# Low parts of weights and activations from Pool to VectorE, and range checks from layer 1 to layer 2

## The chip, the cores and the metric

One core of one Trainium2 chip runs the whole program; the other cores of the chip run nothing of it. The metric is the device time of one execution in microseconds, and a kernel's time is the median of its runs. TensorE (PE in the profile), VectorE (DVE), ScalarE (ACT), GpSimd (POOL, called Pool here) and SyncE (SP, which issues the DMAs) each work through a queue of their own in order and wait for one another by semaphores. TensorE's granted clock is printed as a share of full speed: 1.00 is 2.4 GHz, 0.50 is 1.2 GHz.

## The reference

A recurrence over 768 tokens (4 batches, 8 heads of 48 columns) gives the input of two layers of 384 to 2048 to 384 columns each, one with an ELU, one with a sigmoid gate. All of it in float32:

```python
for t in range(S):                                    # attention
    cur = np.einsum('bhd,bhe->bhde', u[None] * kt, vt)
    y[:, :, t] = np.einsum('bhd,bhde->bhe', rt, state + cur)
    state = wt[:, :, :, None] * state + np.einsum('bhd,bhe->bhde', kt, vt)
x = y.transpose(0, 2, 1, 3).reshape(3072, 384)
h = x @ w_in;  x = np.where(h > 0, h, np.exp(np.minimum(h, 0)) - 1) @ w_out     # layer 1
h = x @ w2_in; x = (h * (1 / (1 + np.exp(-1.702 * h)))) @ w2_out                # layer 2
```

The weights arrive as float64, in pairs of 32-bit words.

## The kernel before

**Layers.** The 3072 tokens go in 6 tiles of 512. A layer's 2048 inner columns are 16 blocks of 128 (index f). `layers` runs 192 steps j: first 6 tiles of 16 steps for layer 1 (j from 0 to 95), then the same for layer 2 (96 to 191). Step j issues on TensorE the 9 products of h for block f of its tile (L145) and among them the output products of the block two steps back (9 of layer 1, L176; 12 of layer 2, L185). Each float32 value is used as a high part (rounded by a ScalarE cast) and a low part (the value less its high part): three products stand for one. `split_g` makes the two parts of a step's activation g: the cast is L168, the subtraction L169. h has two PSUM banks, and e, g and hl two buffers each.

**Weights.** One block's weights (in and out, 128x768 pairs of words) are loaded (`load_w`), turned into float32 by bit operations on VectorE (`bits_w`: L100 or L104 and L106, then L110 twice) and split by `parts_w`: cast on ScalarE (L134), subtraction on Pool (L135). Layer 1's 16 blocks are made in the first tile, two steps ahead of their use; two of them before the first step, beside the attention's first chunks (`lead`). Layer 2's take their places and are made from step `turn` = 82 on, at 8/3 VectorE operations a step.

**Range checks.** Layer 1's weights are made as if all were in float32's range. That is checked later: half blocks are loaded again (`see`, L115 to L117) and looked at by one ScalarE square and three VectorE passes (`check`, L124 to L128), one half a step, in steps 5 to 15 of layer 1's later tiles. Layer 2's weights are checked as they are made: a ScalarE square with an accumulator (L87), a compare (L104) and a masked shift (L106). The decays are checked by `flags`, two ScalarE passes a chunk with accumulators (L262, L263), while the chunk's decays lie in memory. All leave their results in the columns of two small tiles, which `verdict` sums up once in layer 2; a second path for any inputs (`any_decay`) would run after it and does not with these inputs.

**Attention.** 24 chunks of 128 tokens, four stages each, one stage a step beside layer 1; four chunks and a stage come before the first step. Pool makes keys, queries and bonus products (L270, L278, L330, L331, L343) and a key's low part (L306); VectorE the scans (L242, L249), masks and state.

**The order** is written out by hand (a manual schedule): what a step's code issues in this order goes into each engine's queue in this order.

```python
        issue(mm, among, late)                       # TensorE: the step's products
        if j >= 1:
            making = j <= NF or j >= turn and state["parts"] < len(order)
            hls[j - 1] = moe.split_g(gs.pop(j - 1), TILE, nc.gpsimd if making else nc.vector)
```

Then come the step's share of the weights, `soon` (attention), `act` (the activation of h), `after` (attention, or the verdict), `parts_w` in the first tile, `see` and `check`, and at a tile's second step the copies of the finished tile out of PSUM (L514 in layer 1; in layer 2 L523, two on VectorE and two on ScalarE, each followed by its DMA). Layer 2's next input is loaded at f = 3 to 5 and split at f = 4 to 6.

Of the kernel before, what the change touches and what calls it, by code (L numbers as in the profile page):

```python
# [12 lines left out]
F32 = mybir.dt.float32  # L13
# [38 lines left out]
class Moe:  # L52
    """Two products with an activation between them, tokens along the free dimension."""
# [11 lines left out]
    # float64 weights, as pairs of words, to the high and the low part of a float32.  # L65
    #
    # A float64's high word holds sign, 11 bits of exponent and 20 of mantissa. In the range of
    # normal float32 numbers its exponent's bits 9 to 7 are all the opposite of bit 10, so taking
    # them out and moving the rest leaves the float32. As float32 patterns the high words are in
    # order of size: one comparison of squares finds those below the range, of which no bits are  # L70
    # moved; numbers above it are clamped, or counted for the caller.

    def later(self, layer):
        return self.large is not None and layer == 1

    def sq_w(self, layer, f):
        nc = self.nc
        if self.later(layer):
            return
        hf = self.raw[layer, f][:, 1].bitcast(F32)  # L80
        t = self.t[layer, f] = self.p["tmp"].tile([P, 2 * DM], F32, tag="tmp", name="wt")
        if self.large is None:
            nc.vector.tensor_scalar(out=hf, in0=hf, scalar1=-HIGH_MAX, scalar2=HIGH_MAX, op0=ALU.max, op1=ALU.min)
            nc.scalar.activation(t, hf, AF.Square)
        else:
            i = 2 * NF + f
            nc.scalar.activation(t, hf, AF.Square, accum_out=self.large[:, i:i + 1])  # L87
# [3 lines left out]
    def bits_w(self, layer, f):  # L91
# [3 lines left out]
        if self.later(layer):  # L95
            t = self.t[layer, f] = self.p["tmp"].tile([P, 2 * DM], F32, tag="tmp", name="wt")
        t = self.t[layer, f]
        ti = t.bitcast(I32)
        if self.later(layer):
# [12 lines left out]
    # The first layer's weights are made in a hurry, as if all were in the range or zeros. That is  # L112
    # looked after later, half a block at a time.

    def see(self, src, k):  # L115
        raw = self.t["seen", k] = self.p["tmp"].tile([P, 2 * DM], I32, tag="tmp", name="seen")
        self.nc.sync.dma_start(raw, src[k // 2][:, k % 2 * 2 * DM:(k % 2 + 1) * 2 * DM])  # L117
# [12 lines left out]
    def parts_w(self, layer, f):  # L130
# [4 lines left out]
        nc.gpsimd.tensor_tensor(out=w[:, 1, :], in0=t, in1=w[:, 0, :].bitcast(F32), op=ALU.subtract)  # L135

    def h(self, layer, f, x, n):
        """PSUM [f rows, tokens] of x @ w_in, and the products that fill it."""
# [11 lines left out]
    def act(self, layer, h, n):  # L150
# [3 lines left out]
        if layer == 1:  # L154
            # exp(min(h, 0)) - 1 = -relu(1 - exp(h)); elu = max of it and h
# [9 lines left out]
    def split_g(self, g, n, engine):  # L165
# [3 lines left out]
        engine.tensor_tensor(out=hl[:, 1, :n], in0=g[:, :n], in1=hl[:, 0, :n].bitcast(F32), op=ALU.subtract)  # L169
# [25 lines left out]
class Attention:  # L195
    """A chunk of tokens at a time, all heads. With E the decays' product before a token and I
    with its own, token t takes r_t E_t . (k_s / I_s) of v_s from the tokens s of its chunk, and
    r_t E_t of the state before the chunk; the state after it is I of the last token times what
    (k / I)^T v adds up to. The flags tell where the decays leave the bounds in which no product
    of a chunk can leave the range of float32."""  # L200
# [14 lines left out]
    def room(self, c, what, rows, cols):  # L215
        """For what is loaded; before the layers, in the places of the last of their weights."""
# [9 lines left out]
    def psum(self, what):  # L226
        """A bank; the second layer's tags are free as long as there is only attention."""
# [7 lines left out]
    def decay(self, c):  # L235
        """Products of the decays, in both directions."""
# [15 lines left out]

    def flags(self, c):
        if c >= NCH or "flags" in self.t[c]:
            return
        nc = self.nc
        self.t[c]["flags"] = True
        w = self.t[c]["w"][:, :NP * SEG].rearrange("p (s t) -> p s t", t=SEG)[:, :, 1:]
# [22 lines left out]
    def block(self, c, copy=None):  # L281
        """The queries of each head apart from those of the other one of its pair, in their parts once
        the weights are made."""
# [185 lines left out]
def layers(nc, moe, w1, w2, x2d, out, x_of, beside, lead):  # L469
# [67 lines left out]
    for j in range(STEPS):  # L537
# [27 lines left out]
        if moe.large is not None and NF < j < turn and f >= CALM and seen <= 2 * NF:  # L565
            # in the middle of a tile
            if seen < 2 * NF:
                moe.see(w1, seen)
# [317 lines left out]
```

## Time and profile before

Three runs took 1038.16, 1040.42 and 1041.01 us, median 1040.42. One execution was profiled; its instructions span 1036.9 us (its time outside the span is not recorded, the runs' times hold it).

| | |
|---|---|
| time, median of 3 | 1040.42 us |
| span of the profiled execution | 1036.9 us |
| TensorE busy | 978.0 us, 94% |
| its weight loads | 831.6 us, 80% |
| VectorE | 700.7 us, 68% |
| ScalarE | 457.3 us, 44% |
| Pool | 313.0 us, 30% |
| subtractions for weights' low parts, Pool, L135 | 32 of 2120 ns |
| for activations' low parts, L169 | 44 on Pool of 1670 ns, 148 on VectorE of 742 ns |
| checks of weights, `seen` loads | 32 of 384 KB, 3.4 us to landing |

A share of the whole span says little here, since the program runs through stretches with different limits: the table of stretches in the rows below gives each engine's busy time in microseconds, and how near that is to the length of the stretch. The list of groups gives for each line and shape a count, the busy time and the mean duration; where that mean is well above the shortest of the same shape, something held the instruction.

### The profile page before, as it was taken

To read this page: it belongs to the slowest core of one execution; us is meant where nothing else is said; L and a number is where in the kernel's file an instruction comes from. 1 tells how busy PE (TensorE), PEld (TensorE's weight loads), DVE (VectorE), ACT (ScalarE), POOL (GpSimd) and SP (SyncE) were. 2 spreads that over 40 slices of the span, in tenths; PEclk is the share of its full clock that TensorE was granted. 3 is DMA by queue.
4 is the path that set the end of the run, shared out by engine and by line. 5 is a ranking of instruction groups with operands and counts; after the bars stand their busy time and mean duration, and the time that the engine had idled before them with its cause. 6 is when DMAs were issued, how large, how long until landed. Compare 5 with 4: busy or idle time off the path is not lost.

```text
span 1036.9 us, 12859 instructions
## 1 busy us (share of the span) xinstructions
PE 978.0 (94%) x4895; PEld 831.6 (80%) x4895; DVE 700.7 (68%) x946; ACT 457.3 (44%) x854; POOL 313.0 (30%) x223
## 2 busy tenths in 40 slices
PE   7898887999999999999999999899999999999997
PEld 5676665787878878887888777789999999899996
DVE  7999997689969978996743989954334343343332
ACT  4344334454655555565535665433233332332322
POOL 5667865333332322423302665720000000000000
PEclk9787998999999999999999999999999999999999
DMA  9744311224333422432004542001010010100000
GB/s 238 219 172 168 115 40 40 81 88 129 127 119 112 125 96 80 138 111 85 19 1 160 198 160 92 0 3 60 1 61 1 1 61 1 60 3 1 31 1 34
DMA packets 27670, 83.74 MB, mean 81 GB/s; under 512 B 3152, under 2 KB 6352, under 8 KB 27600
## 3 DMA queue, kind: packets, MB, share of 16 engines
q1 hardware_dynamic: 27600, 82.84, 25.2%
q8 instruction: 40, 0.66, 0.3%
q14 instruction: 30, 0.25, 0.1%
HBM read 73.39 MB, written 9.44 MB: 80 GB/s over the span
## 4 chain that ended last, share of the span: by engine, by line
PE 66%; DVE 18%; issue 7%; ACT 3%; POOL 3%; DMA 2%; SPq 0%; DVEq 0%; ACTq 0%; POOLq 0%
PE h L145 29%; PE o L185 17%; PE o L176 13%; DVE wt L110 6%; PE py L450 3%; PE pa L450 2%; DVE g L158 2%; DVE wt L100 1%; DVE parts L294 1%; DMA lent<-in_rkw 1%; DVE e L242 1%; ACT e L157 1%; DVE wt L106 1%; DVE g L162 1%; ACT e L156 1%
## 5 line engine op out<-in xcount | busy, mean ns | idle before, releaser
L145 PE MATMUL h<-xt,w 128*128 128x512 f32 x1728 | 476.9, 406 | 22.7 <-POOL w L135 9.6
L145 PEld LDWEIGHTS h<-xt,w 128*128 128x128 f32 x1728 | 320.0, 191 | 89.9 <-POOL w L135 12.7
L176 PE MATMUL o<-hl,w 128*128 128x512 f32 x864 | 280.2, 427 | 8.3 <-DVE x L514 7.9
L185 PE MATMUL o<-w,hl 128*128 128x384 f32 x1152 | 218.6, 338 | 0.5
L185 PEld LDWEIGHTS o<-w,hl 128*128 128x128 f32 x1152 | 204.2, 188 | 10.8 <-POOL hl L169 1.8
L168 ACT CAST hl<-g 128x512 fp32r<-128x512 f32 x192 | 118.9, 619 | 210.8 <-PE o L185 107.6
L176 PEld LDWEIGHTS o<-hl,w 128*128 128x128 f32 x864 | 157.8, 193 | 37.1 <-DVE x L514 9.3
L169 DVE TENSOR_TENSOR hl<-g,hl 128x512 fp32r<-128x512 f32 x148 | 109.8, 742 | 106.6 <-ACT hl L168 106.3
L162 DVE TENSOR_TENSOR g<-e,h 128x512 f32<-128x512 f32 x96 | 65.9, 686 | 117.2 <-ACT e L161 117.2
L110 DVE SCALAR_TENSOR_TENSOR wt<-raw,wt 128x768 int32<-128x768 int32 x64 | 119.5, 1867 | 1.9
L161 ACT ACTIVATE e<-h 128x512 f32<-128x512 f32 x96 | 57.2, 596 | 121.1 <-PE h L145 121.0
L169 POOL TENSOR_TENSOR hl<-g,hl 128x512 fp32r<-128x512 f32 x44 | 73.5, 1670 | 90.9 <-ACT hl L168 90.9
L158 DVE SCALAR_TENSOR_TENSOR g<-e,h 128x512 f32<-128x512 f32 x96 | 65.4, 681 | 50.2 <-ACT e L157 46.1
L135 POOL TENSOR_TENSOR w<-wt,w 128x768 fp32r<-128x768 f32 x32 | 67.9, 2120 | 20.3 <-ACT w L134 20.2
L156 ACT ACTIVATE e<-h 128x512 f32<-128x512 f32 x96 | 57.0, 593 | 31.7 <-PE h L145 31.7
L450 PEld LDWEIGHTS py<-tok,at 128*128 128x128 f32 x304 | 59.7, 198 | 10.7 <-issue 0.8
L157 ACT ACTIVATE e<-e 128x512 f32<-128x512 f32 x96 | 60.6, 632 | 3.1
L270 POOL TENSOR_TENSOR kh<-kr,gi 112x512 f32<-112x512 f32 x19 | 27.5, 1449 | 111.5 <-issue 85.4
L450 PE MATMUL pa<-parts,khl 112*128 112x256 f32 x192 | 55.4, 288 | 5.4 <-DVE parts L294 5.4
L450 PE MATMUL py<-tok,at 128*128 128x48 f32 x304 | 49.9, 247 | 0.7 <-DVE at L375 0.3
L375 DVE COPY_PREDICATED at<-mask,pa 128x512 f32<-128x512 int32 x48 | 32.3, 727 | 23.9 <-PE pa L450 22.0
L134 ACT CAST w<-wt 128x768 fp32r<-128x768 f32 x32 | 26.6, 832 | 49.4 <-DVE wt L110 49.4
(120 smaller groups left out, 939.9 us busy)
## 6 DMA issues: line engine op xcount, KB each, us to landing
raw<-in_w SPq DMA_DIRECT2D x32, 768.0 KB, 4.6
seen<-in_w SPq DMA_DIRECT2D x32, 384.0 KB, 3.4
tok<-in_tok SPq DMA_DIRECT2D x20, 576.0 KB, 4.5
kr<-in_rkw SPq DMA_DIRECT2D x20, 448.0 KB, 4.4
x2d<-x SPq DMA_DIRECT2D x18, 256.0 KB, 2.4
x<-x2d SPq DMA_DIRECT2D x18, 256.0 KB, 3.6
w<-in_rkw SPq DMA_DIRECT2D x20, 226.2 KB, 2.7
lent<-in_tok SPq DMA_DIRECT2D x4, 576.0 KB, 15.3
```

The costliest lines, as they stand in the source:

```text
L110: yield nc.vector.scalar_tensor_tensor(out=ti, in0=a, scalar=n, in1=ti, op0=shift, op1=put)
L135: nc.gpsimd.tensor_tensor(out=w[:, 1, :], in0=t, in1=w[:, 0, :].bitcast(F32), op=ALU.subtract)
L145: nc.tensor.matmul(h[:, :n], w[:, a, k * P:(k + 1) * P], x[:, b, k, :n], start=i == 0, stop=i == len(mm) - 1)
L156: nc.scalar.activation(e[:, :n], h[:, :n], AF.Exp)
L157: nc.scalar.activation(e[:, :n], e[:, :n], AF.Relu, bias=1.0, scale=-1.0)
L158: nc.vector.scalar_tensor_tensor(out=g[:, :n], in0=e[:, :n], scalar=-1.0, in1=h[:, :n], op0=ALU.mult, op1=ALU.max)
L162: nc.vector.tensor_tensor(out=g[:, :n], in0=e[:, :n], in1=h[:, :n], op=ALU.mult)
L168: nc.scalar.copy(hl[:, 0, :n], g[:, :n])
L169: engine.tensor_tensor(out=hl[:, 1, :n], in0=g[:, :n], in1=hl[:, 0, :n].bitcast(F32), op=ALU.subtract)
L176: nc.tensor.matmul(acc[d][:, :n], w[:, a, DM + d * P:DM + (d + 1) * P], hl[:, b, :n], start=f == 0 and i == 0, stop=f == NF - 1 and i == 2)
L185: nc.tensor.matmul(acc[s][:, :DM], hl[:, b, s * P:(s + 1) * P], w[:, a, DM:2 * DM], start=f == 0 and i == 0, stop=f == NF - 1 and i == 2)
L450: b[done]()
```

## The change

1. `parts_w` and `split_g` subtract on VectorE always; Pool keeps the attention alone.
2. Layer 2's weights are made on the same short path as layer 1's (no square, no compare). `bits_w` takes L100's form for both.
3. No check is done in layer 1. From step `CALM` = 112 on, one step's half block of either layer's weights is loaded again and checked, 64 halves in 65 steps (32 before).
4. The decays are loaded again in the same stretch, a chunk every second step, and `flags` reads them from there, 24 chunks, in place of its four calls beside layer 1 and ahead of it (the `see` with one argument in the diff is the attention's); the small tiles get 64 columns, and the verdict moves from step 160 to 178.

Comments are dropped, and lines have other numbers by a few; names are the same.

```diff
     @property
     def later(self):
         return self.large is not None
...
     def see(self, src, k):
         raw = self.t["seen", k] = self.p["tmp"].tile([P, 2 * DM], I32, tag="tmp", name="seen")
-        self.nc.sync.dma_start(raw, src[k // 2][:, k % 2 * 2 * DM:(k % 2 + 1) * 2 * DM])
+        i = k // 2
+        self.nc.sync.dma_start(raw, src[i // NF][i % NF][:, k % 2 * 2 * DM:(k % 2 + 1) * 2 * DM])
...
         nc.scalar.copy(w[:, 0, :], t)
-        nc.gpsimd.tensor_tensor(out=w[:, 1, :], in0=t, in1=w[:, 0, :].bitcast(F32), op=ALU.subtract)
+        nc.vector.tensor_tensor(out=w[:, 1, :], in0=t, in1=w[:, 0, :].bitcast(F32), op=ALU.subtract)
...
-    def split_g(self, g, n, engine):
+    def split_g(self, g, n):
...
-        engine.tensor_tensor(out=hl[:, 1, :n], in0=g[:, :n], in1=hl[:, 0, :n].bitcast(F32), op=ALU.subtract)
+        nc.vector.tensor_tensor(out=hl[:, 1, :n], in0=g[:, :n], in1=hl[:, 0, :n].bitcast(F32), op=ALU.subtract)
...
+    def see(self, c):                         
+        t = self.t["seen", c] = self.p.tile([PR, OK], F32, tag=("w", "e", "gi")[c % 3], name="seen")
+        self.nc.sync.dma_start(t, self.rkw_d[c, :, :OK])
     def flags(self, c):
-        w = self.t[c]["w"][:, :NP * SEG].rearrange("p (s t) -> p s t", t=SEG)[:, :, 1:]
+        w = self.t.pop(("seen", c))[:, :NP * SEG].rearrange("p (s t) -> p s t", t=SEG)[:, :, 1:]
...
-            making = j <= NF or j >= turn and state["parts"] < len(order)
-            hls[j - 1] = moe.split_g(gs.pop(j - 1), TILE, nc.gpsimd if making else nc.vector)
+            hls[j - 1] = moe.split_g(gs.pop(j - 1), TILE)
...
-        if moe.large is not None and NF < j < turn and f >= CALM and seen <= 2 * NF:
-            if seen < 2 * NF:
-                moe.see(w1, seen)
-            if seen > 0:
-                moe.check(seen - 1)
-            seen += 1
+        if moe.later and CALM <= j <= CALM + CHECKS:
+            k = j - CALM
+            if k < CHECKS:
+                moe.see((w1, w2), k)
+            if k > 0:
+                moe.check(k - 1)
...
-                        at.flags(n)
...
-                if j == STEPS - 2 * NF:
+                if j == CALM + CHECKS + 2:
                     return [], 0, lambda: None, lambda: at.verdict(bad)
-                return NOTHING
+                k, odd = divmod(j - CALM, 2)
+                def decays():
+                    if k < NCH:
+                        at.see(k)
+                    if k > 0:
+                        at.flags(k - 1)
+                return ([], 0, lambda: None, decays) if 0 <= k <= NCH and odd else NOTHING
```

How the queues stand, at three places. VectorE in the first tile, two steps of the kernel before (wt is a weight being made, x at L397 the attention's output of a chunk, g a step's activation):

```order
L158 SCALAR_TENSOR_TENSOR g<-e,h 128x512
L397 TENSOR_TENSOR x<-tok,py 128x384
L100 TENSOR_SCALAR wt<-raw_681 128x768
L110 SCALAR_TENSOR_TENSOR wt<-raw_681,wt 128x768 x2
L158 SCALAR_TENSOR_TENSOR g<-e,h 128x512
L290 COPY x_89<-r 48x4x128 x2
```

The same place after it:

```order
L397 TENSOR_TENSOR x<-tok,py 128x384
L133 TENSOR_TENSOR w_793<-wt,w_793 128x768
L167 TENSOR_TENSOR hl<-g,hl 128x512
L97 TENSOR_SCALAR wt<-raw_663 128x768
L107 SCALAR_TENSOR_TENSOR wt<-raw_663,wt 128x768 x2
L156 SCALAR_TENSOR_TENSOR g<-e,h 128x512
L290 COPY x_89<-r 48x4x128 x2
L133 TENSOR_TENSOR w_833<-wt,w_833 128x768
```

Each step has a weight's subtraction (L133) behind the chunk's work and an activation's (L167) behind that. ScalarE in layer 2, around the step in which a tile's sums leave PSUM (L523), before:

```order
L168 CAST hl<-g 128x512
L161 ACTIVATE e<-h 128x512
L523 COPY x_89<-o_5795 128x384
L523 COPY x_89<-o_5797 128x384
L168 CAST hl<-g 128x512
```

and after:

```order
L166 CAST hl<-g 128x512
L159 ACTIVATE e<-h 128x512
L262 ACTIVATE junk,flag<-seen,wmin 112x512
L263 ACTIVATE junk,flag<-seen,wmax 112x512
L122 ACTIVATE checked,large<-seen 128x384
L524 COPY x_89<-o_5478 128x384
L524 COPY x_89<-o_5480 128x384
L166 CAST hl<-g 128x512
```

Two flags passes and the check's square stand between the sigmoid and the copies. VectorE at the same step, before:

```order
L169 TENSOR_TENSOR hl<-g,hl 128x512
L162 TENSOR_TENSOR g<-e,h 128x512
L523 COPY osb<-o_5794 128x384
L523 COPY osb<-o_5796 128x384
L169 TENSOR_TENSOR hl<-g,hl 128x512
```

and after:

```order
L167 TENSOR_TENSOR hl<-g,hl 128x512
L160 TENSOR_TENSOR g<-e,h 128x512
L123 TENSOR_SCALAR checked<-checked 128x384
L124 SCALAR_TENSOR_TENSOR checked<-seen,checked 128x384
L126 TENSOR_REDUCE flag<-checked 128x1
L524 COPY osb<-o_5477 128x384
L524 COPY osb<-o_5479 128x384
L167 TENSOR_TENSOR hl<-g,hl 128x512
```

The three passes of a check, which read what ScalarE's square wrote, stand ahead of the copies.

## Rows read from the trace of the kernel before

**Rows 1.** Table of stretches: start:end, length, busy us of each engine (instructions), clock, DMA.

```profile
48.00:165.00 117.00, 98.53 (x434) 77.37 (x434) 112.46 (x115) 47.86 (x85) 82.45 (x50) 0.87 0.34 118
165.00:200.00 35.00, 29.18 (x141) 23.81 (x140) 23.84 (x32) 14.81 (x28) 16.38 (x13) 0.90 0.19 60
200.00:560.00 360.00, 351.73 (x1873) 294.78 (x1873) 284.07 (x443) 193.78 (x392) 106.20 (x86) 1.00 0.30 93
560.00:690.00 130.00, 119.39 (x542) 98.01 (x541) 114.28 (x101) 70.24 (x125) 78.42 (x42) 1.00 0.32 110
690.00:1037.00 347.00, 340.20 (x1713) 308.32 (x1711) 124.77 (x190) 109.51 (x185) 0.00 (x0) 1.00 0.07 24
```

**Rows 2.** Time order, VectorE and Pool in the first tile: start, us, instruction.

```profile
101.44 2.12 POOL L135 TENSOR_TENSOR w<-wt,w 128x768 fp32r<-128x768 f32 x1 [2.75 <-ACT w L134]
...
101.89 2.09 DVE L100 TENSOR_SCALAR wt<-raw 128x768 int32<-128x768 int32 x1
```

**Rows 3.** Durations of the tile wt: count, minimum/median/maximum in ns.

```profile
L110 DVE SCALAR_TENSOR_TENSOR wt<-raw,wt x64: 947/1933/2581, 28.8 to 679.0; 128x768 int32<-128x768 int32 x64
...
L100 DVE TENSOR_SCALAR wt<-raw x16: 542/868/2220, 28.2 to 157.9; 128x768 int32<-128x768 int32 x16
```

**Rows 4.** Groups on VectorE, 48 to 165 us: count, busy us, mean ns, idle before.

```profile
L110 DVE SCALAR_TENSOR_TENSOR wt<-raw,wt 128x768 int32<-128x768 int32 x29 | 49.6, 1711 | 1.0
L100 DVE TENSOR_SCALAR wt<-raw 128x768 int32<-128x768 int32 x14 | 17.4, 1245 | 0.2
L242 DVE TENSOR_TENSOR_SCAN e<-w,sep 112x516 f32<-112x516 f32 x4 | 9.5, 2384 | 0.0
```

**Rows 5.** Durations at two lines, 48 to 165 us: minimum/median/maximum.

```profile
L290 DVE COPY x<-r x4: 411/909/1801, 101.0 to 133.9; 48x512 f32<-48x512 f32 x4
...
L245 DVE COPY last<-e x4: 170/1066/1070, 48.0 to 150.0; 112x4 f32<-112x4 f32 x4
```

**Rows 6.** Groups on VectorE, 200 to 560 us, the scan.

```profile
L242 DVE TENSOR_TENSOR_SCAN e<-w,sep 112x516 f32<-112x516 f32 x14 | 17.2, 1225 | 0.0
```

**Rows 7.** Groups on Pool, 48 to 165 us, the two that move.

```profile
L135 POOL TENSOR_TENSOR w<-wt,w 128x768 fp32r<-128x768 f32 x15 | 30.1, 2007 | 20.3 <-ACT w L134 20.2
L169 POOL TENSOR_TENSOR hl<-g,hl 128x512 fp32r<-128x512 f32 x13 | 23.5, 1810 | 0.0
```

**Rows 8.** Durations at L169 where VectorE runs it, whole span.

```profile
L169 DVE TENSOR_TENSOR hl<-g,hl x148: 680/692/1433, 185.3 to 1026.7; 128x512 fp32r<-128x512 f32 x148
```

**Rows 9.** Groups on VectorE, 560 to 690 us, the weights' passes.

```profile
L110 DVE SCALAR_TENSOR_TENSOR wt<-raw,wt 128x768 int32<-128x768 int32 x32 | 65.6, 2051 | 0.8
L106 DVE SCALAR_TENSOR_TENSOR wt<-raw,wt 128x768 int32<-128x768 int32 x16 | 16.2, 1013 | 0.3
```

**Rows 10.** Durations of the tile checked, all 32 checks.

```profile
L124 ACT ACTIVATE checked<-seen x32: 530/551/567, 220.0 to 457.4; 128x384 f32<-128x384 f32 x32
L124 ACT ACTIVATION_READ_ACCUMULATOR checked<-seen x32: 185/188/198, 220.4 to 457.9; 128x1 f32 x32
L125 DVE TENSOR_SCALAR checked<-checked x32: 348/353/1074, 222.0 to 459.5; 128x384 f32<-128x384 f32 x32
L126 DVE SCALAR_TENSOR_TENSOR checked<-seen,checked x32: 557/1067/1434, 222.4 to 459.9; 128x384 int32<-128x384 int32 x32
L128 DVE TENSOR_REDUCE flag<-checked x32: 552/553/554, 223.5 to 461.4; 128x1 f32<-128x384 int32 x32
```

**Rows 11.** Durations at L262, one of a chunk's two flags passes.

```profile
L262 ACT ACTIVATE junk<-w,wmin x20: 705/707/722, 8.3 to 503.4; 112x512 bf16<-112x512 f32 x20
```

**Rows 12.** Time order in layer 2, the step in which a tile's sums are copied.

```profile
763.84 2.27 PE L185 MATMUL o<-w,hl 128*128 128x384 f32 x12
764.10 0.60 ACT L161 ACTIVATE e<-h 128x512 f32<-128x512 f32 x1 [1.52 <-PE h L145]
...
765.33 1.01 DVE L523 COPY osb<-o 128x384 f32<-128x384 f32 x2
...
768.02 2.27 PE L185 MATMUL o<-w,hl 128*128 128x384 f32 x12
```

More of the change, by code (lines that the diff above doesn't have):

```diff
@@ L63, in load_w, with later @@
         self.nc.sync.dma_start(raw, src[f])
-    def later(self, layer):
-        return self.large is not None and layer == 1
+    @property
+    def later(self):
+        return self.large is not None
     def sq_w(self, layer, f):
         nc = self.nc
-        if self.later(layer):
+        if self.later:
             return
@@ L81, in sq_w @@
         t = self.t[layer, f] = self.p["tmp"].tile([P, 2 * DM], F32, tag="tmp", name="wt")
[L82 to L87, printed above, removed]
+        nc.vector.tensor_scalar(out=hf, in0=hf, scalar1=-HIGH_MAX, scalar2=HIGH_MAX, op0=ALU.max, op1=ALU.min)
+        nc.scalar.activation(t, hf, AF.Square)
     large = small = None
@@ L94, in bits_w @@
         low, high = words[:, 0], words[:, 1]
-        if self.later(layer):
+        if self.later:
             t = self.t[layer, f] = self.p["tmp"].tile([P, 2 * DM], F32, tag="tmp", name="wt")
@@ L98, in bits_w @@
         ti = t.bitcast(I32)
-        if self.later(layer):
+        if self.later:
             yield nc.vector.tensor_scalar(out=ti, in0=high, scalar1=3, scalar2=0x3FFFFFF8,
@@ L251, in decay @@
         nc.vector.memset(sep[:, SEG::SEG], 1.0)
+    def see(self, c):
+        t = self.t["seen", c] = self.p.tile([PR, OK], F32, tag=("w", "e", "gi")[c % 3], name="seen")
+        self.nc.sync.dma_start(t, self.rkw_d[c, :, :OK])
     def flags(self, c):
-        if c >= NCH or "flags" in self.t[c]:
-            return
         nc = self.nc
-        self.t[c]["flags"] = True
-        w = self.t[c]["w"][:, :NP * SEG].rearrange("p (s t) -> p s t", t=SEG)[:, :, 1:]
+        w = self.t.pop(("seen", c))[:, :NP * SEG].rearrange("p (s t) -> p s t", t=SEG)[:, :, 1:]
         junk = self.p.tile([P, NP * PR], F32, tag="kt", name="junk", bufs=2).bitcast(BF16)[:PR, :NP * C]
@@ L310, in verdict @@
         nc = self.nc
-        large = self.p.tile([P, 3 * NF], F32, tag="rk", name="large")
+        large = self.p.tile([P, CHECKS], F32, tag="rk", name="large")
         s = self.p.tile([P, 2], F32, tag="q", name="s")
@@ L457 @@
 TILE = 512
-CALM = 5
 LATE = (0, 6, 2, 6)
@@ L466 @@
 STEPS = 2 * NTILE * NF
+CHECKS = 4 * NF
+CALM = 112
 def layers(nc, moe, w1, w2, x2d, out, x_of, beside, lead):
@@ L533, in make_x2 @@
         split(nc, xs[2, i][:, :, d, :], xs.pop(("raw", i, d)))
-    seen = 0
     lead(take)
@@ L581, in layers @@
     j = STEPS
-    hls[j - 1] = moe.split_g(gs.pop(j - 1), TILE, nc.vector)
+    hls[j - 1] = moe.split_g(gs.pop(j - 1), TILE)
     issue(finish_pe(j - 2), [])
@@ L591, in constants @@
     nc.vector.memset(c["busy"], 1.0)
-    flag = c["flag"] = pool.tile([P, 2 * NCH + 2 * NF], F32, tag="flag", name="flag")
+    flag = c["flag"] = pool.tile([P, 2 * NCH + CHECKS], F32, tag="flag", name="flag")
     nc.gpsimd.memset(flag, 0.0)
-    c["large"] = pool.tile([P, 3 * NF], F32, tag="large", name="large")
+    c["large"] = pool.tile([P, CHECKS], F32, tag="large", name="large")
     ident = c["ident"] = pool.tile([P, P], F32, tag="ident", name="ident")
@@ L702, in lead @@
                 at.block(0, (nc.scalar.copy, nc.vector.tensor_copy))
-                at.flags(0)
                 at.warm(WARM[0])
@@ L712, in lead @@
                 at.block(1)
-                at.flags(1)
                 for c in range(per):
@@ L744, in lead @@
                     at.block(c + 2)
-                    at.flags(c + 2)
                 take("load", 5)
```

## The prediction

> **What bounds the kernel now.** I read the table of stretches first [rows 1]. It cuts the span where the work changes: 48 to 165 us is the first tile, in which layer 1's weights are still being made; 200 to 560 us is layer 1 with its weights ready; 560 to 690 us is the turn, in which layer 2's weights are made; from 690 us on it is layer 2 alone. The reader is to compare the busy times with the stretch's length. In the first tile VectorE is busy 112.46 of 117 us, TensorE 98.53 at a granted clock of 0.87: VectorE sets the pace. In layer 1 TensorE is busy 351.73 of 360 us, so 8.3 us is all that can be won there. In the turn TensorE lacks 10.6 of 130 us while VectorE has 114.28: both are near the bound. In layer 2 TensorE sets the pace (340.20 of 347, the rest being the tail), VectorE has 124.77 and Pool nothing. What the change does is therefore worth something different in each stretch, and a sum over the whole span would mislead.
>
> Next I looked at what VectorE's time in the first tile consists of. A piece of the time order shows the mask pass L100 taking 2.09 us while Pool's weight subtraction of 2.12 us runs [rows 2]; over the kernel the same form takes 0.542 us at least, and the word passes L110 run from 0.947 to 2.581 us with one shape [rows 3]. So VectorE is slow beside Pool, and a subtraction that leaves Pool gives VectorE back some of what it costs there.
>
> **First tile, the subtractions.** Added to VectorE between 48 and 165 us: 15 weight subtractions of 128x768 (Pool ran 15 [rows 7]) at 0.947 us, the undisturbed time of another two-input pass of that shape [rows 3], 14.2 us; and 13 activation subtractions [rows 7] at 0.692 us, VectorE's own time for it [rows 8], 9.0 us. Together 23.2 us, and nothing hides them: VectorE is the bound, so that is also what they cost if Pool's share gave nothing back. Given back: the passes over their undisturbed times, from the means of the stretch. L110, 29 x (1.711 - 0.947) = 22.2; L100, 14 x (1.245 - 0.542) = 9.8 [rows 3, 4]; the scan L242, 4 x (2.384 - 1.225) = 4.6 [rows 4, 6]; L290, 4 x (0.909 - 0.411) = 2.0, and L245, three of four at 0.9 too much, 2.7 [rows 5]. That is 41.3 us in which VectorE was held. Pool was busy 82.45 us [rows 1], of which the two moved groups are 30.1 + 23.5 = 53.6 us [rows 7], 65%. By that share 26.8 us comes back. Net 23.2 - 26.8 = -3.6; I take **-4**. The ends are -18 (all 41.3 comes back, 23.2 is paid) and +23 (nothing does). The value taken is nearer to the first since the two moved groups are also the longest Pool operations. The order on VectorE hides the new waits: the weight subtraction stands behind the chunk's own work and the activation's behind that, so ScalarE's two casts run meanwhile.
>
> The rule of the Trainium skill that bears on this, "SBUF — State Buffer", section "Who interferes with whom", has VectorE and GpSimd share one port pair under an exclusive lock, the loser fully blocked for the other's whole instruction. The 2.09 us of [rows 2] fit that. It also speaks against the share above, since by it every Pool operation that is left can still hold VectorE for its whole length; the sum would then be +10 in place of -4, which is rival C.
>
> **First tile, the rest.** Pool keeps the attention's products; its queue is emptied of the moved ones, so these come earlier, but nothing waited for them once VectorE was the bound. The decay flags (two ScalarE passes of 0.707 us each [rows 11], with two accumulator reads like the check's 0.188 [rows 10], 1.8 us a chunk) leave ScalarE, which had 47.86 of 117 us [rows 1]: nothing, the cover being VectorE. The two weights made before 48 us move likewise, one for one: nothing, at worst two subtractions, 2 us. From 165 to 200 us TensorE lacks 5.8 us [rows 1] while the same passes run out: **-1**, between 0 and -3.
>
> **Layer 1, 200 to 560 us.** 32 checks leave: on VectorE 0.353 + 1.067 + 0.553 = 2.0 us each, on ScalarE 0.551 + 0.188 [rows 10], and the flags with them. VectorE had 284.07 of 360 us [rows 1], so it was not the bound but late at times. At most the 8.3 us that TensorE lacks come back; some of it belongs to attention stages that stay. I take **-3**, ends 0 and -7.
>
> **The turn, 560 to 690 us.** Pool has only the 16 weight and 26 activation subtractions here, so after the change it has nothing and VectorE runs undisturbed. Gone: 32 x (2.051 - 0.947) = 35.3 us of L110 and the 16.2 us of L106, which the shorter path without range test does not issue [rows 9] (a compare pass goes too and is left as margin). New: 16 x 0.947 + 16 x 0.542 for L100 + 26 x 0.692 = 41.8 us. VectorE goes from 114.3 to 104.6 us of 130 or lower. That is not the whole gain of 10.6: the activation's subtraction now stands on VectorE right behind the product of the same step, and between the two lies ScalarE's cast, a pass of the sigmoid's size, 0.60 us [rows 12], in which VectorE has nothing else in its queue. Per step that is two thirds of a weight (0.542 + 3 x 0.947) = 2.26, the product 0.69, the subtraction 0.69 and the pause 0.60: 4.24 us, against TensorE's step of 768.02 - 763.84 = 4.18 [rows 12]. The two are level, and the loads of layer 2's input come on top. I take half, **-5**, ends 0 and -10.
>
> **Layer 2, from 690 us.** 64 checks and 24 flags arrive where TensorE sets the pace, in steps 112 to 176, with their loads: 64 halves of 384 KB and 24 decays of 226 KB, 31 MB in 64 steps of 4.18 us or some 115 GB/s, what the first tile moves now (118 GB/s [rows 1]). On SyncE's queue they stand ahead of the next input's loads, which are needed ten steps later. VectorE: 124.77 of 347 us is 36%, 1.5 us a step; a check without Pool is 0.348 + 0.557 + 0.552 = 1.46 [rows 10]; 3.0 of 4.18. ScalarE: 109.51 of 347 is 1.3 us a step; the square 0.74 and every second step the flags' 1.8; 2.9 of 4.18. An activation is needed two steps after its product, so a step that runs late is made good: nothing, on all but the last step of a tile. There the copies out of PSUM stand behind the check on VectorE, and the check behind the flags on ScalarE. Now the sigmoid ends at 764.70 us and TensorE starts on those banks at 768.02 [rows 12]; after it 764.70 + 1.8 + 0.55 + 0.19 + 1.46 + 0.5 for the first of two copies (1.01 for both) = 769.2. TensorE waits 1.2 us. That holds for three tile turns (at the first the flags have not begun, after the third they are done): **+4**, ends 0 and +10 if the next loads, which need the same buffers, are late too.
>
> **The sum** is -4 - 1 - 3 - 5 + 4 = -9 on a span of 1036.9 us, the one profiled execution; that lies 3.5 us under the median of the three runs, 1040.42, for what is around the span, and I carry the 3.5 over: 1031.5.
>
> **Rivals.** *B, VectorE gets back more:* all 41.3 us in the first tile, and TensorE keeps its pace in the turn. For it: the moved operations are Pool's longest. Against: a third of Pool's work stays. First tile -15, then -2, -5, -9, +3: 1040.4 - 28 = 1012. *C, slower, the attention's Pool operations hold VectorE:* 82.45 - 53.6 = 28.8 us of Pool work stays in the first tile, beside a VectorE with more two-input passes than before. If each holds it for its whole length, 28.8 us is lost there and not the 14.5 that are its share now: +14, 1045.5. It turns slower than before once the loss there is over 14.5 + 9 = 23.5 us. For it: the 2.09 beside 2.12 us [rows 2]. Against: only half of Pool's busy time (41.3 of 82.45) shows up as such loss now. *D, slower, the checks set the pace of layer 2:* if a check takes what it takes in layer 1 (2.0 and not 1.46 us [rows 10]), a pair of steps with flags, in which ScalarE and VectorE wait for each other, goes a microsecond past TensorE's 8.4; 24 such pairs less some 5 us of slack, +19 in place of +4: 1046.5. Against: Pool is idle there. *E, no change:* the first tile costs what the turn and layer 1 give: 1040.
>
> **Chances.** Forecast 0.46 (its own range 1024 to 1037), B 0.20, C 0.13, D 0.09, E 0.12. A measurement of this kernel tells about 0.3%, 3.1 us, from no change. Faster: 0.46 + 0.20 = 0.66; the same 0.12; slower 0.13 + 0.09 = 0.22. The range takes in the forecast, C, D, E and the greater part of B: 1014 to 1048.
>
> **What would show it.** In the profile after: L110's counterpart near 1.3 us in the first tile (1.7 under C, 1.0 under B) and at 0.95 in the turn; the first tile's last weight at about 161 us and not 165; TensorE's idle time in the turn halved; in layer 2 VectorE at about 72% in the checked steps, and TensorE waiting for a copy at three tile turns, some 1.2 us each. The prediction is wrong if VectorE idles before the new subtractions in the first tile, or if TensorE waits in ordinary steps of layer 2.

## The result, and the profile after

The changed kernel took 1015.78 us (median of 4 runs, 1009.45 to 1019.38) against 1040.72 us for the kernel before beside it: a ratio of 0.975, 95% interval 0.972 to 0.979. A second measurement beside the last experiments gave 1011.8 us and 0.972 (0.970 to 0.974). Faster, as forecast, but by 25 to 29 us and not by 9.

The profiled execution took 1009.45 us, the fastest of the four, so its stretches add up to more than the medians' 25 us; its span is 1007.2 us. Its table of stretches, cut near where the same steps fall (columns as in [rows 1]):

```profile
48.00:153.00 105.00, 91.86 (x423) 73.50 (x423) 102.02 (x139) 40.68 (x67) 33.22 (x23) 0.90 0.37 128
153.00:185.00 32.00, 28.51 (x152) 23.42 (x151) 24.84 (x39) 14.38 (x25) 11.32 (x9) 1.00 0.23 76
185.00:540.00 355.00, 350.82 (x1872) 295.70 (x1870) 236.63 (x349) 157.85 (x271) 106.95 (x85) 1.00 0.18 59
540.00:657.00 117.00, 116.02 (x546) 99.91 (x545) 92.81 (x128) 56.50 (x93) 0.00 (x0) 1.00 0.38 130
657.00:1008.00 351.00, 340.61 (x1711) 307.63 (x1709) 209.83 (x381) 177.01 (x409) 0.00 (x0) 0.99 0.34 108
```

Against the lengths of [rows 1], 117, 35, 360, 130 and 347 us, that is -12, -3, -5, -13 and +4, where -4, -1, -3, -5 and +4 were forecast. (Cut at exactly the same steps, as in the next section, the first tile is 12.5 us shorter, layer 1 5.7, the turn 14.0, and layer 2 is 2.9 longer.) The first tile and the turn hold 16 of the 20 us that were missed. In the first tile VectorE (third pair of columns) is still the bound, 102.02 of 105 us; in the turn TensorE now is, 116.02 of 117.

Groups of instructions on VectorE in 48 to 153 us (as in [rows 4]: count, busy us, mean ns, idle before):

```profile
L107 DVE SCALAR_TENSOR_TENSOR wt<-raw,wt 128x768 int32<-128x768 int32 x29 | 32.7, 1129 | 1.0
L167 DVE TENSOR_TENSOR hl<-g,hl 128x512 fp32r<-128x512 f32 x13 | 13.8, 1058 | 0.0
L133 DVE TENSOR_TENSOR w<-wt,w 128x768 fp32r<-128x768 f32 x14 | 13.3, 951 | 0.5 <-ACT w L132 0.3
L97 DVE TENSOR_SCALAR wt<-raw 128x768 int32<-128x768 int32 x14 | 10.7, 761 | 0.0
L240 DVE TENSOR_TENSOR_SCAN e<-w,sep 112x516 f32<-112x516 f32 x4 | 4.9, 1223 | 0.0
```

L107 is the L110 of [rows 4]: 1711 to 1129 ns; L97 is L100: 1245 to 761; the scan L240 is L242: 2384 to 1223. The new subtractions, L133 and L167, wait for ScalarE 0.3 us in all. In the turn (from the gate product g of step 82 to that of step 112):

```profile
L107 DVE SCALAR_TENSOR_TENSOR wt<-raw,wt 128x768 int32<-128x768 int32 x32 | 30.6, 955 | 0.5
L167 DVE TENSOR_TENSOR hl<-g,hl 128x512 fp32r<-128x512 f32 x30 | 20.8, 692 | 18.3 <-ACT hl L166 17.8
L133 DVE TENSOR_TENSOR w<-wt,w 128x768 fp32r<-128x768 f32 x16 | 15.3, 959 | 0.7
L97 DVE TENSOR_SCALAR wt<-raw 128x768 int32<-128x768 int32 x16 | 8.9, 554 | 0.0
```

The 2051 ns of [rows 9] are 955, and the pause behind ScalarE's cast is there, 17.8 us in 30 steps, 0.6 each. And at a tile turn of layer 2 (time order, as in [rows 12]):

```profile
731.23 0.71 ACT L262 ACTIVATE junk<-seen,wmin 112x512 bf16<-112x512 f32 x1
...
732.78 0.53 ACT L122 ACTIVATE checked<-seen 128x384 f32<-128x384 f32 x1
...
734.42 0.55 DVE L126 TENSOR_REDUCE flag<-checked 128x1 f32<-128x384 int32 x1
...
734.89 1.01 DVE L524 COPY osb<-o 128x384 f32<-128x384 f32 x2
...
735.59 2.33 PE L183 MATMUL o<-w,hl 128*128 128x384 f32 x12 [0.71 <-ACT e L159]
```

Flags, square, three passes, then the copy: the order that the prediction drew. The first of the two copies ends at about 735.4 and TensorE starts at 735.59, 0.71 us late. The sigmoid of the next step, which the profile names as releaser, ends at about the same time (735.52 us); it had waited for TensorE's own h and not for a check, and the wait is gone in the two experiments on layer 2 below, which points to the copy.

### The profile page after: what moved, and what is told of

It reads as the page before. It is cut to its first block, busy times and chain, and to the rows that moved or that the text cites. A ratio compares the mean times of both kernels' runs of the same rounds, so it can differ in the third digit from the quotient of the medians.

```text
span 1007.2 us, 13002 instructions
## 1 busy us (share of the span) xinstructions
PE 966.6 (96%) x4895; PEld 829.3 (82%) x4895; DVE 707.3 (70%) x1102; ACT 459.6 (46%) x886; POOL 179.5 (18%) x147
## 4 chain that ended last, share of the span: by engine, by line
PE 78%; DVE 14%; issue 3%; POOL 2%; ACT 1%; DMA 0%; ACTq 0%; POOLq 0%; DVEq 0%
PE h L143 34%; PE o L183 20%; PE o L174 16%; DVE wt L107 4%; PE py L450 3%; PE pa L450 2%; DVE w L133 2%; DVE hl L167 1%; DVE wt L97 1%; DVE g L156 1%; PE pd L450 1%; DVE parts L294 1%; DVE e L240 1%; DVE gi L247 1%; ACT w L132 1%
## 5 line engine op out<-in xcount | busy, mean ns | idle before, releaser
L143 PE MATMUL h<-xt,w 128*128 128x512 f32 x1728 | 469.4, 401 | 4.2 <-DVE w L133 3.0
L167 DVE TENSOR_TENSOR hl<-g,hl 128x512 fp32r<-128x512 f32 x192 | 150.2, 783 | 43.7 <-ACT hl L166 42.4
L107 DVE SCALAR_TENSOR_TENSOR wt<-raw,wt 128x768 int32<-128x768 int32 x64 | 67.5, 1055 | 1.6
L270 POOL TENSOR_TENSOR kh<-kr,gi 112x512 f32<-112x512 f32 x19 | 31.6, 1661 | 150.1 <-issue 133.0
L123 DVE TENSOR_SCALAR checked<-checked 128x384 f32<-128x384 f32 x64 | 22.8, 356 | 39.7 <-ACT checked L122 39.7
L378 ACT COPY kt<-pk 128x448 f32<-128x448 f32 x20 | 10.7, 534 | 86.2 <-PE pk L450 64.0
```

What stands on the lines that cost most here:

```text
L107: yield nc.vector.scalar_tensor_tensor(out=ti, in0=a, scalar=n, in1=ti, op0=shift, op1=put)
L143: nc.tensor.matmul(h[:, :n], w[:, a, k * P:(k + 1) * P], x[:, b, k, :n], start=i == 0, stop=i == len(mm) - 1)
L167: nc.vector.tensor_tensor(out=hl[:, 1, :n], in0=g[:, :n], in1=hl[:, 0, :n].bitcast(F32), op=ALU.subtract)
```

## The experiments

All stretches below are cut at the start of the gate product g in steps 0, 16, 82, 112 and 191 of the profiled execution, to a tenth of a microsecond. Those that the same code fills differ between executions by up to 2.7 us in the first tile and 4.7 in layer 1; in the turn and in layer 2 they repeat within 0.5 us.

| kernel | first tile 0-16 | layer 1 16-82 | turn 82-112 | layer 2 112-191 | median, us |
|---|---|---|---|---|---|
| before | 120.9 | 370.9 | 138.8 | 331.1 | 1040.7 |
| after | 108.4 | 365.2 | 124.8 | 334.0 | 1015.8; 1011.8 |
| subtractions alone | 108.4 | 371.8 | 139.3 | 331.1 | 1032.2 |
| checks alone | 121.1 | 366.4 | 123.3 | 333.9 | 1020.9 |
| Pool beside | 140.5 | 366.7 | 164.0 | 333.9 | 1087.4 |
| no checks | 110.9 | 366.7 | 125.2 | 331.1 | 1011.3 |
| VectorE pass back | 109.9 | 365.3 | 139.1 | 333.9 | 1027.5 |
| ScalarE square back | 108.4 | 365.2 | 125.2 | 333.9 | 1013.0 |
| weights only | 119.7 | 366.4 | 130.5 | 333.9 | 1026.4 |
| activations only | 119.1 | 365.2 | 125.8 | 334.0 | 1024.0 |
| attention on VectorE | 107.9 | 368.3 | 124.9 | 333.9 | 1013.7 |
| tile turns free | 110.9 | 366.8 | 125.3 | 331.1 | 1012.1 |
| combined | 109.8 | 363.6 | 123.3 | 331.1 | 1006.5 |

### The two halves of the change

The kernel before with the subtractions moved:

```diff
-        nc.gpsimd.tensor_tensor(out=w[:, 1, :], in0=t, ...)
+        nc.vector.tensor_tensor(out=w[:, 1, :], in0=t, ...)
...
-            hls[j - 1] = moe.split_g(gs.pop(j - 1), TILE, nc.gpsimd if making else nc.vector)
+            hls[j - 1] = moe.split_g(gs.pop(j - 1), TILE, nc.vector)
```

> The kernel before with the two kinds of subtractions on VectorE and nothing else changed. H (the hold: a Pool subtraction holds VectorE for nearly its whole length, so moving it gives back more than it costs): the first tile is some 12 us shorter, the short passes L110 fall from 1.71 to 1.1 us there; in the turn the 16 masked shifts L106 stay, 15 us of VectorE at 0.95 us, so only about half of the turn's 13 us comes, -6; with -3 behind the first tile the sum is -21, 1019 us. W (the work that left: the gain came from the checks of layer 1 and the shorter path of layer 2's weights): first tile -4 as forecast, turn -2, 1034 us.

Measured 1032.16 us, ratio 0.992 (0.990 to 0.995). Stretches, the first tile and the turn:

```profile
64.10:172.50 108.40, 96.81 (x437) 77.35 (x436) 103.12 (x143) 49.09 (x88) 28.26 (x19) 0.91 0.36 125
544.30:683.60 139.30, 128.22 (x583) 105.55 (x582) 110.80 (x148) 73.72 (x130) 0.00 (x0) 1.00 0.31 108
```

Its groups on VectorE in the turn:

```profile
L110 DVE SCALAR_TENSOR_TENSOR wt<-raw,wt 128x768 int32<-128x768 int32 x32 | 30.6, 956 | 0.8
L169 DVE TENSOR_TENSOR hl<-g,hl 128x512 fp32r<-128x512 f32 x30 | 20.8, 692 | 18.3 <-ACT hl L168 17.7
...
L106 DVE SCALAR_TENSOR_TENSOR wt<-raw,wt 128x768 int32<-128x768 int32 x16 | 15.3, 956 | 0.3
```

The first tile is exactly that of after, and there H holds. In the turn it fails: L110 gives 35 us back, the subtractions and their pauses take them again, and the stretch stays at 139 us (138.8 before). So the total is near W's 1034 us and not H's 1019. The gain in the turn belongs to something else.

The kernel after with the subtractions back on Pool:

```diff
+        nc.gpsimd.tensor_tensor(out=w[:, 1, :], in0=t, ...)
...
+            making = j <= NF or j >= turn and state["parts"] < len(order)
+            hls[j - 1] = moe.split_g(gs.pop(j - 1), TILE, nc.gpsimd if making else nc.vector)
```

> The kernel after with the subtractions back on Pool where they were; the checks are all in layer 2 and layer 2's weights take the short path. H: first tile as before (within 2 us), layer 1 -4, the turn -6 at most since L110 stays near 2.05 us there, layer 2 +4: 1034 us, and together with the other half it makes up the whole gain. W: layer 1 and turn give most of the gain, 1020 us.

Measured 1020.91 us, 0.981 (0.979 to 0.983). The first tile and the turn, and the turn's passes:

```profile
62.00:183.10 121.10, 95.95 (x442) 73.42 (x441) 111.93 (x113) 43.42 (x72) 82.56 (x50) 0.94 0.27 95
549.50:672.80 123.30, 123.30 (x582) 106.81 (x581) 95.03 (x88) 60.80 (x98) 77.15 (x43) 1.00 0.38 130
```

```profile
L107 DVE SCALAR_TENSOR_TENSOR wt<-raw,wt 128x768 int32<-128x768 int32 x32 | 53.0, 1656 | 0.6
L97 DVE TENSOR_SCALAR wt<-raw 128x768 int32<-128x768 int32 x16 | 16.7, 1043 | 0.0
```

The turn falls by 15.5 us to TensorE's own pace, 123.30 of 123.30, although Pool still holds VectorE's passes at 1656 ns. W's total was right here, 1020 us, and H's 1034 wrong. So some two thirds of the gain (19.7 us by the medians) are the shorter path and the moved checks, one third (8.5 us) the subtractions, and these in the first tile alone.

### Does Pool hold VectorE at all

After, with Pool doing the same subtractions once more:

```diff
         nc.vector.tensor_tensor(out=w[:, 1, :], in0=t, ...)
+        nc.gpsimd.tensor_tensor(out=t, in0=t, in1=w[:, 0, :].bitcast(F32), op=ALU.subtract)
...
+        if making:
+            nc.gpsimd.tensor_tensor(out=g[:, :n], in0=g[:, :n], in1=hl[:, 0, :n].bitcast(F32), op=ALU.subtract)
```

> The kernel after, VectorE's work unchanged, and Pool does the same subtractions once more where it did them before (results written over inputs that are no longer needed, and read by nobody). H: the hold comes back on top of VectorE's own subtractions, 41 less some 13 us in the first tile and 20 to 30 us of passes in the turn, of which TensorE feels some 12: about 1055 us, slower than the kernel before. W: nothing waits for Pool's copies, so within 5 us of the kernel after, 1016 to 1021 us.

Measured 1087.35 us, 1.045 (1.042 to 1.047). First tile and turn; one of its passes in the first tile; TensorE's waits in the turn (us in total, times, longest):

```profile
67.10:207.60 140.50, 111.14 (x434) 86.40 (x433) 132.55 (x143) 43.63 (x72) 84.20 (x48) 0.79 0.20 73
574.30:738.30 164.00, 138.18 (x583) 113.32 (x582) 135.37 (x132) 59.73 (x98) 89.25 (x43) 0.93 0.29 98
```

```profile
L97 DVE TENSOR_SCALAR wt<-raw 128x768 int32<-128x768 int32 x13 | 28.4, 2183 | 0.0
```

```profile
PE h L144 <- DVE g L161: 16.2, 8, 3.1
PE h L144 <- DVE g L157: 9.5, 6, 3.1
```

The same VectorE instructions are busy 132.55 us in the first tile where after has 103.12, and 135.37 in the turn where it has 95.41; L97 takes 2183 ns. VectorE waits for Pool only once in the two stretches (3.8 us, for a bonus product), so it is its passes that are longer: the hold is real. In the first tile it is near H's price (29.4 us, where 41 less 13 was expected), in the turn larger (40.0, where 20 to 30 was). The whole time holds more than that: TensorE, busy 111.14 of 140.5 and 138.18 of 164.0 us, was also granted a lower clock in the two stretches, 0.79 and 0.93 in the mean (1.00 and 0.50 are its two levels) against 0.92 and 1.00 in the kernel after.

### What the turn gained from

The short path took away one VectorE pass (L106) and one ScalarE square (L87) for each of layer 2's weights. Each was put back alone:

```diff
-            yield None
+            yield (nc.vector.scalar_tensor_tensor(out=ti, in0=high, scalar=3, in1=ti, op0=ALU.logical_shift_left,
+                                                  op1=ALU.bitwise_and) if layer == 2 else None)
```

> The kernel after with one more VectorE pass for each of layer 2's 16 weights, a repeated shift and mask with the same result, where the masked shift L106 stood; no square and no compare. V (what the turn won came from VectorE's 16 passes of 0.95 us, since its passes, the pauses of 0.6 us and the products made the step longer than TensorE's): the turn, 111 us from step 82 to 108 in the kernel after, is some 13 us longer, layer 2's stretch as after: 1029 us. S (it came from ScalarE's 16 squares of some 0.85 us, which stood ahead of the cast or the sigmoid): no longer than after by 3 us, 1016 us.

```diff
         if self.later:
+            if layer == 2:
+                t = self.t[layer, f] = self.p["tmp"].tile([P, 2 * DM], F32, tag="tmp", name="wt")
+                nc.scalar.activation(t, self.raw[layer, f][:, 1].bitcast(F32), AF.Square)
             return
...
-        if self.later:
+        if self.later and layer == 1:
```

> The kernel after with ScalarE's square of each of layer 2's 16 weights back in its place (its result is overwritten by the shift); VectorE's passes as after, and the shift waits for the square. V: within 3 us of the kernel after, 1016 us. S: the turn some 13 us longer, 1029 us.

The pass: 1027.46 us, 0.988 (0.984 to 0.991). The square: 1013.03 us, 0.975 (0.973 to 0.978). VectorE's group with the pass and TensorE's waits, then ScalarE's group with the square, all in the turn:

```profile
L99 DVE SCALAR_TENSOR_TENSOR wt<-raw,wt 128x768 int32<-128x768 int32 x16 | 15.3, 956 | 0.3
```

```profile
PE h L144 <- DVE g L161: 5.8, 4, 1.5
PE h L144 <- DVE g L157: 3.0, 2, 1.5
```

```profile
L82 ACT ACTIVATE wt<-raw 128x768 f32<-128x768 f32 x16 | 14.5, 907 | 0.0
```

15.3 us of passes make the turn 14.3 us longer (139.1 against 124.8) and bring back TensorE's waits for the gate product, which frees the banks of h; 14.5 us of squares cost nothing (125.2 against 124.8, within the 0.5 us by which the turn repeats). V is shown: after stands at the point where VectorE's chain and TensorE's step are level, and there each microsecond added to VectorE counts almost whole. A shorter chain on VectorE gives little more: with the subtractions, and so their pauses, on Pool the turn is 123.3 us.

### One kind of subtraction alone

After, with the activations' subtractions back on Pool where they were:

```diff
+            making = j <= NF or j >= turn and state["parts"] < len(order)
+            hls[j - 1] = moe.split_g(gs.pop(j - 1), TILE, nc.gpsimd if making else nc.vector)
```

> The kernel after with only the weights' subtractions on VectorE; the activations' stay on Pool in the first tile and the turn. In the first tile (step 0 to 16, 121 us before and 108 after), if the hold goes with Pool's busy time: 13 us are added and half of 36 comes back, -5: 116 us there and 1016 to 1018 us in all. If Pool's subtraction of an activation is what VectorE stood behind (its idle time of some 5 us before g goes with it as well): only -2, 119 us and 1019 us. The turn stays bound by TensorE, as after.

And with the weights':

```diff
-        nc.vector.tensor_tensor(out=w[:, 1, :], in0=t, ...)
+        nc.gpsimd.tensor_tensor(out=w[:, 1, :], in0=t, ...)
```

> The kernel after with only the activations' subtractions on VectorE; the weights' stay on Pool. If the hold goes with Pool's busy time: 16 us are added in the first tile and half of 36 comes back, with a part of the idle time -4: 117 us there and 1017 us in all. If the activation's subtraction on Pool was the costly one: -9 there, 112 us and 1012 us.

Measured 1026.35 us, 0.987 (0.985 to 0.989), and 1024.02 us, 0.985 (0.982 to 0.988): each alone is no faster than none (1020.91, 0.981), the first slower, and both together are faster. The first tile of the first, stretch and passes, and of the second:

```profile
61.50:181.20 119.70, 100.17 (x447) 78.27 (x446) 110.57 (x127) 43.33 (x72) 51.70 (x36) 0.89 0.26 95
```

```profile
L107 DVE SCALAR_TENSOR_TENSOR wt<-raw,wt 128x768 int32<-128x768 int32 x27 | 33.7, 1249 | 0.9
L97 DVE TENSOR_SCALAR wt<-raw 128x768 int32<-128x768 int32 x13 | 19.1, 1473 | 0.0
```

```profile
64.40:183.50 119.10, 97.65 (x441) 76.11 (x440) 110.91 (x128) 43.70 (x72) 52.64 (x34) 0.91 0.26 92
```

```profile
L107 DVE SCALAR_TENSOR_TENSOR wt<-raw,wt 128x768 int32<-128x768 int32 x27 | 34.2, 1265 | 0.9
L167 DVE TENSOR_TENSOR hl<-g,hl 128x512 fp32r<-128x512 f32 x16 | 18.7, 1170 | 1.7 <-ACT hl L166 1.4
```

VectorE is busy 111.93 us with both on Pool, 110.57 and 110.91 with one, 103.12 with none. The first 30 us taken from Pool give back what they cost and some 1 us more; the second 24 give 7.5 us over their cost. In the first tile each alone gave -1.4 and -2.0 us, both -12.7. So the split by Pool's busy time (-5, -4) is wrong, and the other reading too: the weights came out as it says (119 us), but the activations then had to give -9. In the turn the weights alone are 7 us slower than none moved: their subtraction then stands right behind ScalarE's cast and VectorE waits 22.1 us for it:

```profile
L133 DVE TENSOR_TENSOR w<-wt,w 128x768 fp32r<-128x768 f32 x16 | 22.8, 1422 | 22.1 <-ACT w L132 22.1
```

Another reading of the first tile, that TensorE and not VectorE had stood behind Pool's low parts of weights (it waited 9.6 us for them before and 13.1 with the subtractions back on Pool), does not hold: with the weights' subtractions alone on VectorE TensorE waits 5.7 us for VectorE's in their place, and the tile is still 119.7 us.

The attention's products of four chunks on VectorE as well, so that Pool is idle in the first tile (shown for the keys; queries, bonus and key parts likewise):

```diff
-        (engine or nc.gpsimd).tensor_tensor(out=kh, ...)
+        (engine or (nc.vector if 5 <= c <= 8 else nc.gpsimd)).tensor_tensor(out=kh, ...)
```

> The kernel after with the attention's products of chunks 5 to 8, those made beside the first tile's steps, on VectorE too, so that Pool is idle there. Added per chunk: two products of 0.69 and three of 0.54 us, 12 us in all and one low part. If what Pool still does holds VectorE for about as long as VectorE needs to do it (12 us above the undisturbed times are left): first tile 108 within 3 us, the whole as after. If the rest holds it for its whole length (28.7 us of Pool, rival C's price): 16 us less, 92 us. If it holds little there, since VectorE reads PSUM or is past it: 8 to 12 us longer.

Measured 1013.69 us, 0.974 (0.972 to 0.977), as after beside it (1011.8, intervals overlapping). First tile:

```profile
63.40:171.30 107.90, 97.73 (x441) 79.71 (x440) 102.22 (x162) 44.30 (x72) 0.61 (x1) 0.89 0.28 100
```

```profile
L107 DVE SCALAR_TENSOR_TENSOR wt<-raw,wt 128x768 int32<-128x768 int32 x27 | 25.9, 958 | 0.9
...
L167 DVE TENSOR_TENSOR hl<-g,hl 128x512 fp32r<-128x512 f32 x16 | 10.9, 684 | 0.0
L97 DVE TENSOR_SCALAR wt<-raw 128x768 int32<-128x768 int32 x13 | 7.2, 551 | 0.0
```

Every pass is at its undisturbed time, 19 more instructions are on VectorE, and its busy time is 102.22 us against 103.12. What was left of the hold was worth just what Pool's remaining work costs on VectorE; a loss of their whole length, rival C, is refuted.

### Layer 2, and a version that combines the findings

```diff
-        if moe.later and CALM <= j <= CALM + CHECKS:
+        if False:
...
-                return ([], 0, lambda: None, decays) if 0 <= k <= NCH and odd else NOTHING
+                return NOTHING
```

(`large`, which no check fills then, is set to zero once.)

> The kernel after without any check of weights or decays and without their loads (that part of the computation is left out). If the checks cost TensorE only its waits at three tile turns and the few steps behind them, as forecast (+4): 1012 us. If every checked step is slower (8 steps of 34.4 in place of 33.5 us in eight such groups): 1008 us. If they are hidden wholly: 1016 us.

The second edit keeps all checks and takes them off two steps of each tile:

```diff
+BUSY = (1, 2)
+SEEN = [j for j in range(CALM, STEPS) if j % NF not in BUSY][:CHECKS + 1]
...
-        if moe.later and CALM <= j <= CALM + CHECKS:
-            k = j - CALM
+        if moe.later and j in SEEN:
+            k = SEEN.index(j)
```

(the flags likewise; the verdict moves back with the last check.)

> The kernel after with no check, no flags and none of their loads in the second and third step of a tile, the stretch of checks being longer for it. If layer 2's +2.8 us are the tile turns, where copies stand behind a check and the check behind the flags: layer 2 from step 112 falls from 333.9 to 331.1 us, as in the kernel without checks, and the whole by 3 us. If the output's transfers, which hold the buffers that the checks need, only move the wait to a later step: 333 us, no change.

Without checks: 1011.3 us, 0.971 (0.968 to 0.974). With the tile turns free: 1012.13 us, 0.972 (0.970 to 0.974), as after beside it (0.972, 0.970 to 0.974). Layer 2 is 331.1 us in both, 2.8 us less than after and what it was before: the checks cost TensorE the three tile turns, 0.9 us each, and nothing in any other step. The stretch with the tile turns free, all checks kept, has no idle time of TensorE:

```profile
668.50:999.60 331.10, 331.10 (x1665) 299.81 (x1664) 206.88 (x377) 174.64 (x404) 0.00 (x0) 1.00 0.36 114
```

In the whole time 2.8 us can't be told from the spread.

The combined version frees the tile turns, leaves the turn's subtractions on Pool, and lets ScalarE make the block copies of the chunks in the first tile:

```diff
-                (copy or 2 * (nc.scalar.copy if self.alone else nc.vector.tensor_copy,))[j](
+                (copy or 2 * (nc.scalar.copy,))[j](
...
-        nc.vector.tensor_tensor(out=w[:, 1, :], in0=t, ...)
+        (nc.gpsimd if self.later and layer == 2 else nc.vector).tensor_tensor(out=w[:, 1, :], in0=t, ...)
...
+            making = j >= turn and state["parts"] < len(order)
+            hls[j - 1] = moe.split_g(gs.pop(j - 1), TILE, nc.gpsimd if making else nc.vector)
```

> The tile turns free of checks, the turn's subtractions (layer 2's weights, and activations while these are made) back on Pool, the first tile's on VectorE, and the block copies of the chunks in the first tile on ScalarE. By the stretches measured so far: first tile 108.4 less 1.7 of copies, turn 123.3 in place of 124.9, layer 2 331.1 in place of 333.9: 6 us less than the kernel after, 1010 us. If the turn is bound by TensorE either way and the copies were hidden: only layer 2's 3 us, 1013 us.

Measured 1006.45 us, 0.968 (0.965 to 0.970), the fastest here: 5.4 us under after beside it, where 6 were worked out; the two intervals just touch. The turn (123.3) and layer 2 (331.1) are as expected, 4.3 us together. VectorE is busy 1.6 us less in the first tile (101.46 against 103.05 in after beside it), since its copies left it, but the tile (109.8) is not shorter, so a gain from them is not shown.

The unchanged kernel after ran beside these three:

> The kernel after, unchanged, beside the next three on the same chip: about 1016 us, with 108 us from step 0 to 16, 365 from there to 82, 125 to 112 and 333.9 to 191.

Measured 1011.8 us, with stretches of 108.3, 366.8, 124.8 and 333.9 us: the stretches repeat, the median came out 4 us lower.

## Why the prediction was right in direction and wrong in size, and in the turn in cause

**First tile, -4 forecast, -12 measured.** The mechanism was right, the size was not; the mis-sized term is the 26.8 us given back. Pool's busy share (65%) was the wrong measure. Over the undisturbed times of [rows 3] only 29 x (1.129 - 0.947) + 14 x (0.761 - 0.542) = 8.3 us are left on the old passes; of the other three groups nothing to speak of. So 33 of the 41.3 came back, 80%, at a cost of 27.1 us (L133 and L167) and not 23.2, since the new subtractions are held too: L167 took 1.06 us where [rows 8] gave 0.69. That is -6 on VectorE. By steps 0 to 16, VectorE's busy time fell by 9.7 us (112.8 to 103.1) and its idle time by 2.8. Two groups that the prediction had not counted gave a part of the first, the state's product L418 (3.7 to 1.8 us) and the queries' low parts L294 (3.0 to 1.4). The idle time's part is a single wait of VectorE, for the scores' products of one chunk, before and after:

```profile
DVE at L375 <- PE pa L450: 4.1, 1, 4.1
```

```profile
DVE at L375 <- PE pa L450: 1.3, 1, 1.3
```

After the change three of the new subtractions (0.96, 0.68 and 0.68 us) run between L294 and that wait: "nothing hides them" was wrong there. L110's counterpart came out at 1.13 us, between my 1.3 and B's 1.0; the last weight's subtraction began at 157.5 us, where I had put about 161 (164.9 before, on Pool).

**The turn, -5 forecast, -13 measured: the step that failed.** Two errors. The pause is there and VectorE's chain is level with TensorE's step, as worked out (4.24 and 4.18 us). But level meant that nearly all of TensorE's idle time went, 10.6 to 1.0 us; "I take half" had no ground (that the slack of two steps makes good a few hundredths is my explanation and was not tried). And 10.6 us was no upper end: TensorE's busy time in the turn fell too, from 128.2 to 123.8 us for the same products at the same granted clock (1.00), so the busy time before held more than the products need. The turn, before and after:

```profile
554.80:693.60 138.80, 128.19 (x583) 105.53 (x582) 116.44 (x105) 73.59 (x130) 79.70 (x43) 1.00 0.32 109
535.40:660.20 124.80, 123.82 (x581) 106.50 (x581) 95.41 (x131) 59.56 (x98) 0.00 (x0) 1.00 0.37 129
```

The cause was also misplaced. I read the 35 us on L110 as the main relief; the runs show that the subtractions and their pauses take it up (139.3 us with the subtractions alone), and that L106 alone, 16 passes, decides (124.8 to 139.1 us with it put back). The compare pass that I left out as margin is 9.9 us and pays for the new L100.

**Layer 1 and the rest, -4 forecast, -6 measured** (steps 16 to 82, 370.9 to 365.2 us). Checks alone gave -4.5 there and subtractions alone nothing; right within the spread.

**Layer 2, +4 forecast, +2.8 measured.** Right in place and mechanism: three tile turns, 0.9 us each and not 1.2. VectorE is busy 68% from 700 to 930 us (156.61 of 230), where I had put about 72%. Rival D's waits in ordinary steps are absent.

**The rivals.** B's 1012 us is nearest to the time, but its reason, all 41.3 us back, holds in no stretch as it was put, and half of the measured gain (14 us) comes from L106; that its number fits is luck. C is refuted: 1.13 and not 1.7 us. That my -9 is near what the subtractions alone gave (-8.5) is luck too: they gave it in the first tile alone, where I had put -4, and most of the short path's part (-15.5 in the turn) was missing. A forecast for each half of the change might have shown it.

What stays open: why taking either kind of subtraction from Pool gives the first tile next to nothing and taking both gives 12.7 us. A Pool operation may find another pass to hold as long as there are enough of both; that was not tried apart.

## What to carry to other kernels

Where one engine's work lengthens another's, moving a part of it over can be worth next to nothing and the whole set a good deal, as in the first tile here; so price the move for the whole set and not by shares of busy time. Where one engine's chain is level with the bound engine's step, a pass added to it counts almost whole, while a shorter chain gives little more; and the idle time that a profile shows for the bound engine is not the upper end of the gain. Split a change into its parts and forecast each stretch for each part, since a sum that looks right can credit the wrong one.

## What the runs showed of the hardware

Pool's cost to VectorE was about VectorE's own time for the same operations, or more: with 82.6, 51.7, 28.3 and 0.6 us of Pool work in the first tile, VectorE, which took over what left Pool, was busy 111.9, 110.6, 103.1 and 102.2 us. The first and the last step give about what they cost, the middle one 7.5 us more.

Not every pass is held. The gate product g, which reads one operand from PSUM, took 679 ns in the first tile with Pool's extra subtractions and 680 without, while L97, which reads one operand and that from SBUF, went from 777 to 2183 ns; first the former, then after:

```profile
L157 DVE SCALAR_TENSOR_TENSOR g<-e,h 128x512 f32<-128x512 f32 x17 | 11.5, 679 | 2.1 <-ACT e L156 2.0
```

```profile
L156 DVE SCALAR_TENSOR_TENSOR g<-e,h 128x512 f32<-128x512 f32 x17 | 11.6, 680 | 2.1 <-ACT e L155 2.0
```

The Trainium skill, "SBUF — State Buffer", section "Who interferes with whom", says that a VectorE instruction with at most one SBUF input, outside the two-port modes, does not contend with GpSimd; the 679 and 680 ns agree. Whether L97 runs in such a mode no row here shows. "Perfetto Trace Analysis", section "Optimizing Scalar/DVE Operations", warns that moving work between these two might not help; each kind alone (1026.35 and 1024.02 against 1020.91 us) agrees, both together do not.
